# Fused attention and two FFNs on one core: weight conversion begins every second step, and the early FFN products of two token blocks come in two parts

## The chip, the core and the metric

One core of a Trainium2 chip runs the whole program once per launch. Its engines work beside each other, each through its own instructions in order: TensorE (PE; its weight loads are PEld), VectorE (DVE), ScalarE (ACT), GpSimd (POOL), and SyncE (SP), which here issues every DMA. The metric is the device time of one execution in microseconds (us).

## What is computed

Local-and-global attention, then two feed-forward networks one behind the other, on 4 x 544 tokens of 512 features (cut to what matters):

```python
# attention: 32 global and 512 local tokens, 8 heads of 64, window 32
out_g = sm(scale * q_g @ [k_g, k_l].T) @ [v_g, v_l]
out_l = sm(concat(scale * q_l @ k_g.T, masked(scale * q_l @ k_l.T))) @ [v_g, v_l]
x = concat(out_g, out_l)                    # 2176 tokens x 512
# first FFN, 512 -> 2048 -> 512
x = (max(x @ w_in1, 0) ** 2) @ w_out1
# second FFN, a quotient of polynomials between its products
h = x @ w_in2
g = (a0 + a1*h + a2*h**2 + a3*h**3) / (1 + abs(b0)*abs(h) + abs(b1)*h**2 + 1e-6)
out = g @ w_out2
```

The four FFN weights arrive as float64. Each is turned into two float32r words, a high part and a rest, so that three products stand for one of higher precision.

## The kernel before, in words

**Weight items.** The weights are cut into chunks f = 0 to 15 of 128 hidden features; an item is one half (in or out) of a chunk of one FFN: 64 items, 512 KB each as loaded. `w_load` (line 107) loads one into a buffer S; then `w_abs` (ACT, line 150) writes a buffer T, `w_low` (POOL) scales the low words, and DVE does `w_clamp` (153), `w_shift` (164), `w_sign` (168) and `w_add` (173). An item that stays in SBUF then gets `w_hi` (ACT cast, 186) and `w_lo` (DVE, 193); an item of mode "word" is only written from T to a DRAM scratch by a DMA (line 178). The first 10 items (chunks 0 to 4 of the first FFN, NPRE = 5) stay; the next 12 are of mode "word". These 22 are done during attention. S has three buffers in the pool cvp, and items 3 to 6 take four more that borrow the space of weight chunks 3 and 4. T has four buffers in the pool cv3.

**Ticks.** `cv_tick` (line 237) is the clock of this conversion. Every call adds one to a counter and to the age of each item in work. When the counter reaches `cv["per"]` a new item's load is issued; each operation is issued when the item's age reaches the number in the table OX or OE. Attention runs over steps i = 0 to 40, each ending with some ticks: four up to step 14, from then on 2 + i % 2. With per = 4, one item begins in each of the steps 0 to 14, and later one in 1.6 steps.

**Attention steps.** There are eight half-batches (n = 0 to 7: batch and four heads) of five groups. Step i issues, in order: exponentials (747) of group i + 2, scores `do_S` (733, 754) of group i + 3 with their DVE reductions (739), transposes of q and k for the next half-batch (`prep`, 700), the transposition of probabilities `do_T` (787), the transposition of results into xT (`do_xT`, 853), the product with v (`do_PV`, 827), and the ticks. Loads of q, k and v for later half-batches are issued on SP at fixed positions of a step; the v windows of a half-batch are then shifted by four SBUF-to-SBUF copies (lines 601 to 604).

**Fill jobs.** From step F0 = 11 on, one job of the first FFN goes with each step, to keep TensorE filled: 30 jobs, for six blocks of 256 tokens (a) with the five resident chunks (f). `f_h` (507) does the 12 products of the first matrix, `f_low` the square's rest on DVE, `f_y` (529) the 12 products of the second, one step later, summed in two PSUM banks. At the last chunk of a block both banks are copied to T buffers (line 544, one copy on DVE and one on ACT) and written to a DRAM tensor `park` (545). `f_split` (496) makes the two parts of a block of x, four pairs of an ACT cast and a DVE subtraction (503, 504). Job (a, f) can begin when both items of chunk f are done.

**FFN stage.** After attention, `step` (line 440) runs the rest of both FFNs; the parked sums are read back and added.

**Order.** The schedule is written by hand: each engine runs its instructions in the order of issue above, so a waiting instruction holds up all that stands behind it on its engine. SP issues loads, copies and stores in one such line.

Of the kernel before, what the change touches and what calls it, by code (L numbers as in the profile page):

```python
# [23 lines left out]
def kernel(  # L24
# [19 lines left out]
    T = SL + SG  # L44
# [4 lines left out]
    NK = DM // 128  # L49
# [4 lines left out]
    NPRE, NPART, NSUB = 5, 1536, 256  # L54
# [6 lines left out]
    pe, ve, sc, gp, sy = nc.tensor, nc.vector, nc.scalar, nc.gpsimd, nc.sync  # L61
# [25 lines left out]
    cv3 = ctx.enter_context(tc.tile_pool(name="cv3", bufs=4))  # L87
# [7 lines left out]
    park = drp.tile([128, NK, NPART], F32, name="park")  # L95

    def w_src(ap, ph, half, f, m):

        if half:
            return [(slice(0, 128), ap[f * 128:(f + 1) * 128, :])]  # L100
        c = ap[:, f * 128 * m:(f + 1) * 128 * m]
        if ph:
            return [(slice(0, 128), c.rearrange("(k p) f -> p k f", p=128))]
        v = c.rearrange("(u h d) f -> u d h f", u=2, d=D)
        return [(slice(64 * u, 64 * u + 64), v[u]) for u in range(2)]

    def w_load(it):

        ph, f, half = it["k"]
        ap = ((w_in1, w_out1), (w_in2, w_out2))[ph][half]  # L110
        if it["mode"] == "wide":

            if cv["n"] in (3, 5):
                x = wpre.tile([128, 2, 2, 512], F32R, tag=("w4", "w3")[cv["n"] // 5], name="S4").bitcast(U32)
                cv["S"] = [x[:, z].rearrange("p a c -> p (a c)").rearrange("p (a b) -> p a b", b=2) for z in (1, 0)]
            if 3 <= cv["n"] < 7:
                t = cv["S"].pop()
            else:
                t = cvp.tile([128, 512, 2], U32, tag="S", name="S")
            cv["n"] += 1  # L120
            it["S"] = t
            dst, m = t.rearrange("p a b -> p (a b)"), 2
            ap = ap.bitcast(U32)
        else:
            t = cv3.tile([128, 512], U32, tag="T", name="T").bitcast(F32)
            it["T"] = t
            dst, m = t, 1
            if wide:
                sy.dma_start(dst, scr[ph, f, half])
                return  # L130
        for rows, src in w_src(ap, ph, half, f, m):
            d = dst[rows]
            sy.dma_start(d if half else d.rearrange("p (k f) -> p k f", k=NK), src)
# [89 lines left out]

    OX = dict(abs=8, elow=8, clamp=9, shift=9, sign=9, add=10, hi=16, lo=18)
    OE = dict(abs=4, elow=4, clamp=5, shift=6, sign=6, add=8, hi=11, lo=13)
    OL = dict(abs=2, low=3, clamp=3, shift=4, sign=4, add=5, hi=7, lo=9)
    OS = dict(hi=5, lo=8)
    ORD = ("hi", "add", "lo", "clamp", "shift", "sign", "low", "elow", "abs")  # L230
# [256 lines left out]
    fs = ctx.enter_context(ExitStack())  # L487
# [2 lines left out]
    def fill(i):  # L490
        return fp.tile([128, (10, 4, 2)[i] * NSUB], F32, tag=f"f{i}", name=f"f{i}")

    frows, fturn, fx, fh, fg, fy = [], dict(x=0, h=0), {}, {}, {}, []
    fjobs = [(a, f) for a in range(NPART // NSUB) for f in range(NPRE)]

    def frow(i, r):
        return frows[i][:, NSUB * r:NSUB * r + NSUB]

    def f_split(a, k):
        i = fturn["x"] = (fturn["x"] + 1) % 5  # L500
        hi, lo = [frow(0, 2 * i + z).bitcast(F32R) for z in range(2)]
        src = xT[:, k, NSUB * a:NSUB * a + NSUB]
        sc.copy(hi, src)
        ve.tensor_tensor(out=lo, in0=src, in1=hi.bitcast(F32), op=ALU.subtract)
        fx[a, k] = hi, lo

    def f_h(q):
        a, f = fjobs[q]
        while (0, f, 1) not in done:
            cv_tick(LEFT[1])  # L510
        w, h = wt[0, f], bank("H")[:, 0:NSUB]
        for m, (k, s, t) in enumerate([(k, s, t) for k in range(NK) for s, t in ((0, 0), (1, 0), (0, 1))]):
            pe.matmul(h, w[:, s, 0, 128 * k:128 * k + 128], fx[a, k][t], start=m == 0, stop=m == 3 * NK - 1)  # L513
        if f == NPRE - 1:
            for k in range(NK):
                fx.pop((a, k))
        i = fturn["h"] = (fturn["h"] + 1) % 2
        hi, lo = [frow(1, 2 * i + z).bitcast(F32R) for z in range(2)]
        g = frow(2, i)
        sc.activation(g, h, AF.Relu)  # L520
        sc.activation(hi, g, AF.Square)
        fh[q], fg[q] = (hi, lo), (g, h)
# [4 lines left out]
        ve.tensor_tensor(out=lo, in0=g, in1=hi.bitcast(F32), op=ALU.subtract)  # L527

    def f_y(q):
        a, f = fjobs[q]  # L530
        hi, lo = fh.pop(q)
        w = wt[0, f]
        if f == 0:
            fy[:] = [bank("Y"), bank("Y")]
        ms = range(NK)
        for m, z in [(m, z) for m in ms for z in range(2)] + [(m, 2) for m in ms]:

            pe.matmul(fy[m // 2][:, NSUB * (m % 2):NSUB * (m % 2) + NSUB], w[:, z % 2, 1, 128 * m:128 * m + 128],  # L538
                      (hi, hi, lo)[z], start=f == 0 and z == 0 and m % 2 == 0, stop=f == NPRE - 1 and z == 2,
                      skip_group_check=True)  # L540
        if f == NPRE - 1:
            for i in range(2):
                t = cv3.tile([128, 512], U32, tag="T", name="pk").bitcast(F32)
                (sc.copy if i else ve.tensor_copy)(t, fy[i])
                sy.dma_start(park[:, 2 * i:2 * i + 2, NSUB * a:NSUB * a + NSUB], t.rearrange("p (m t) -> p m t", m=2))


    with ExitStack() as at:
# [69 lines left out]
        for i, pair in enumerate(some):  # L618
            for h in range(4):
                p, m = slice(32 * h, 32 * h + 32), pair[h % 2]  # L620
# [18 lines left out]
        def load_g(i):  # L639
            sy.dma_start(gr[i].rearrange("g (x d) -> g x d", d=D), (q_g, k_g)[i].rearrange("b h g d -> g (b h) d"))  # L640

        for c in "kGqAgKQB":
            if c in "qk":
                load_qk(0, "qk".index(c))
            elif c in "QK":
                load_qk(1, "QK".index(c))
            elif c in "gG":
                load_g("gG".index(c))
            else:
                load_v(0, "ABR".index(c))  # L650
# [61 lines left out]
        F0 = 11  # L712
# [151 lines left out]
        pend = {}  # L864
        cv["at"] = OX

# [11 lines left out]
        for i in range(NS + 1):  # L878
# [4 lines left out]
            for c in (LD0 if n == 0 else LD)[pos] if i < NS else ():  # L883
                if c in "qk":
                    m = n + 2 + (c == "k" and pos == 4)
# [34 lines left out]
            if fq == -1:  # L920
                for k in range(NK):
                    f_split(0, k)
            elif 0 <= fq < len(fjobs) - NPRE:
                a, f = fjobs[fq]
                for k in range(NK):
                    if f == (NPRE - 1 if k else NPRE - 2):
                        f_split(a + 1, k)
            if i == 0:
                prep_g(0)
            if i == 1:  # L930
# [1 line left out]
                sy.dma_start(coef[:, 4:6], b2.rearrange("(o a) -> o a", o=1).to_broadcast([128, 2]))  # L932
            if i == 10:
                sc.activation(coef[:, 6:8], coef[:, 4:6], AF.Abs)
            if i == F0 + NPRE - 1:
                cv["at"] = OE
            for _ in range(4 if i < F0 + NPRE - 1 else 2 + i % 2):
                cv_tick(LEFT[1])
        do_xT(NS - 1)
        f_y(len(fjobs) - 1)  # L940
# [43 lines left out]
```

## Time and profile before

| | us |
|---|---|
| median of 3 runs | 942.24 (941.53 to 942.43) |
| the profiled execution | 942.59 |
| its span, first to last instruction | 940.8 |
| PE busy in the span | 903.2 (96%) |
| DVE busy | 727.1 (77%) |
| ACT busy | 618.5 (66%) |

The span is a little shorter than the execution; 1.8 us lie around it. Busy shares are means over stages with different limits, so the rows below are taken by stage: a row of stage times gives the stretch, then for each engine the busy time and, in brackets, the count of instructions, then the granted share of the TensorE clock, the mean busy share of the 16 DMA engines and what they moved. Engine names with a q (SPq) are of the engine's instruction queue. A note such as [1.44 <-DMA kr] tells for how long the engine had been idle and what released it.

### The profile page before, as it was taken

Reading aid. Unit: us, or ns where it says so; the run is one execution under the profiler, and the core shown is the slowest. Engines: PE = TensorE matmul, PEld = TensorE weight load, DVE = VectorE, ACT = ScalarE, POOL = GpSimd, SP = SyncE. Lnnn points to the kernel's source line nnn. Section 1 sums busy time; section 2 is a strip of 40 time slices with the busy share of each in tenths; the row PEclk is TensorE's granted clock in tenths of the full one; section 3 lists DMA queues with packets and bytes.
Section 4 is the critical chain, followed back from the end, with each engine's and each line's share of the span. In section 5 each row is a group of like instructions: output and inputs, shape, how many; then the busy total and the mean of one; then the engine's idle time right before and its main releaser. Section 6 shows DMA issues by size and latency. Waiting matters only on the chain.

```text
span 940.8 us, 19428 instructions
## 1 busy us (share of the span) xinstructions
PE 903.2 (96%) x7440; PEld 822.5 (87%) x7440; DVE 727.1 (77%) x1731; ACT 618.5 (66%) x1323; POOL 57.7 (6%) x109
## 2 busy tenths in 40 slices
PE   7878889999999999999999999999999999999997
PEld 4657788898999999999999988889889998988875
DVE  3599887765469577586766569989989999989886
ACT  3567475654578554555554557877888788787886
POOL 5233122210000000000000000000000000000000
PEclk9888999999999999999999999999999999999999
DMA  9997788730365264354522540010010010010000
GB/s 177 187 216 166 179 213 204 174 104 25 93 177 157 71 188 157 126 200 157 155 82 79 167 147 1 1 33 1 1 34 1 1 34 1 1 34 1 25 10 23
DMA packets 104301, 89.45 MB, mean 95 GB/s; under 512 B 60176, under 2 KB 87312, under 8 KB 104208
## 3 DMA queue, kind: packets, MB, share of 16 engines
q1 hardware_dynamic: 104208, 88.21, 35.2%
q8 instruction: 58, 0.95, 0.4%
q14 instruction: 35, 0.29, 0.1%
HBM read 62.13 MB, written 19.14 MB: 86 GB/s over the span
## 4 chain that ended last, share of the span: by engine, by line
PE 81%; DVE 10%; ACT 4%; DMA 3%; issue 1%; SPq 1%; ACTq 0%; DVEq 0%
PE S L314 33%; PE y L394 18%; PE y L391 15%; PE H L513 4%; PE Y L538 3%; PE S L733 2%; PE tr L700 1%; PE PV L827 1%; DVE T L168 1%; PE T L787 1%; DVE s L739 1%; DVE T L173 1%; DMA S<-in_moe_w_in_dram 1%; DMA big<-in_v_l_dram 1%; DVE tq L364 1%
## 5 line engine op out<-in xcount | busy, mean ns | idle before, releaser
L314 PE MATMUL S<-big,w 128*128 128x384 f32 (+1 forms) x1776 | 328.8, 326 | 2.1 <-ACT big L296 1.1
L314 PEld LDWEIGHTS S<-big,w 128*128 128x128 f32 x1776 | 296.5, 188 | 9.2 <-DVE ts L354 2.2
L394 PE MATMUL y<-w,big 128*128 128x512 f32 x816 | 209.1, 398 | 4.2 <-ACT big L372 2.9
L394 PEld LDWEIGHTS y<-w,big 128*128 128x128 f32 x816 | 149.3, 188 | 38.2 <-DVE big L373 8.1
L391 PE MATMUL y<-big,w 128*128 128x384 f32 (+1 forms) x912 | 159.6, 324 | 0.6 <-DVE xT L401 0.6
L391 PEld LDWEIGHTS y<-big,w 128*128 128x128 f32 x912 | 149.2, 188 | 1.5 <-DVE xT L401 1.0
L350 ACT ACTIVATE big<-S 128x384 f32<-128x384 f32 (+1 forms) x96 | 45.6, 475 | 75.4 <-PE S L314 72.1
L329 ACT ACTIVATE big<-S 128x384 f32<-128x384 f32 (+1 forms) x76 | 35.6, 468 | 81.9 <-PE S L314 81.9
L337 DVE TENSOR_TENSOR big<-big 128x384 f32<-128x384 f32 (+1 forms) x60 | 31.3, 522 | 71.2 <-ACT big L333 71.2
L353 DVE TENSOR_TENSOR ts<-ts,S 128x384 f32<-128x384 f32 (+1 forms) x96 | 50.9, 530 | 24.3 <-ACT ts L351 24.2
L314 PE MATMUL S<-xm,w 128*128 128x384 f32 (+1 forms) x288 | 67.8, 328 | 0.0
L352 ACT ACTIVATE tq<-big,coef 128x384 f32<-128x384 f32 (+1 forms) x96 | 66.1, 689 | 0.0
L351 ACT ACTIVATE ts<-S,coef 128x384 f32<-128x384 f32 (+1 forms) x96 | 62.5, 651 | 0.0
L354 DVE SCALAR_TENSOR_TENSOR ts<-ts,coef,S 128x384 f32<-128x384 f32 (+1 forms) x96 | 56.9, 593 | 3.4
L333 ACT ACTIVATE big<-big 128x384 fp32r<-128x384 f32 (+1 forms) x76 | 38.3, 504 | 29.6 <-PE y L391 29.1
L314 PEld LDWEIGHTS S<-xm,w 128*128 128x128 f32 x288 | 52.1, 188 | 2.9
L150 ACT ACTIVATE T<-S 128x512 f32<-128x512 f32 x64 | 42.7, 670 | 17.9 <-DMA S<-in_moe_w_in_dram 8.9
L366 DVE SCALAR_TENSOR_TENSOR ts<-tq,ts 128x384 f32<-128x384 f32 (+1 forms) x96 | 51.4, 536 | 3.3
L538 PE MATMUL Y<-f,w 128*128 128x256 f32 x360 | 51.3, 293 | 0.0
L513 PE MATMUL H<-f,w 128*128 128x256 f32 x360 | 51.0, 291 | 0.0
L373 DVE TENSOR_TENSOR big<-ts,big 128x384 fp32r<-128x384 f32 (+1 forms) x96 | 50.8, 529 | 0.2 <-ACT big L372 0.2
L355 DVE TENSOR_TENSOR tq<-tq,big 128x384 f32<-128x384 f32 (+1 forms) x96 | 50.8, 529 | 0.0
(131 smaller groups left out, 1314.2 us busy)
## 6 DMA issues: line engine op xcount, KB each, us to landing
S<-in_moe_w_out_dram SPq DMA_DIRECT2D x32, 512.0 KB, 4.5
S<-in_moe_w_in_dram SPq DMA_DIRECT2D x32, 256.0 KB, 4.5
S<-in_moe_w_in_dram SPq DMA_DIRECT2D x16, 512.0 KB, 4.5
scr<-T SPq DMA_DIRECT2D x24, 256.0 KB, 3.2
T<-scr SPq DMA_DIRECT2D x24, 256.0 KB, 2.7
both<-stg SPq DMA_DIRECT2D x10, 512.0 KB, 3.5
w<-both SPq DMA_DIRECT2D x10, 512.0 KB, 4.4
out_dram<-xT SPq DMA_DIRECT2D x17, 256.0 KB, 2.6
```

The costliest lines, as they stand in the source:

```text
L314: pe.matmul(h, wk[k][s], x[k][t], start=m == 0, stop=m == 3 * NK - 1)
L351: sc.activation(s, h, AF.Identity, scale=coef[:, 3:4], bias=coef[:, 2:3])
L352: sc.activation(q, av, AF.Identity, scale=coef[:, 7:8], bias=coef[:, 6:7])
L353: ve.tensor_tensor(out=s, in0=s, in1=h, op=ALU.mult)
L354: ve.scalar_tensor_tensor(out=s, in0=s, scalar=coef[:, 1:2], in1=h, op0=ALU.add, op1=ALU.mult)
L355: ve.tensor_tensor(out=q, in0=q, in1=av, op=ALU.mult)
L366: ve.scalar_tensor_tensor(out=s, in0=q, scalar=2.0, in1=s, op0=ALU.subtract, op1=ALU.mult, reverse0=True)
L373: ve.tensor_tensor(out=lo, in0=s, in1=hi.bitcast(F32), op=ALU.subtract)
L391: pe.matmul(y[m][:, 0:n], a, x, start=st and z == 0, stop=sp and z == 2)
L394: pe.matmul(y[m], a, x, start=st and z == 0, stop=sp and z == 2)
L513: pe.matmul(h, w[:, s, 0, 128 * k:128 * k + 128], fx[a, k][t], start=m == 0, stop=m == 3 * NK - 1)
L538: pe.matmul(fy[m // 2][:, NSUB * (m % 2):NSUB * (m % 2) + NSUB], w[:, z % 2, 1, 128 * m:128 * m + 128], (hi, hi, lo)[z], start=f == 0 and ...
```

## The change

- Items begin every second step up to step 8 (`per=8`, counter started at 4): items 0 to 4 in steps 0, 2, 4, 6, 8; from then one in each of steps 9 to 13, and from step 14 one in seven ticks. All steps have four ticks. The tables OX and OE get shorter ages, and OE holds from step 11. The last item's load is issued in step 34 instead of 25.
- The four borrowed S buffers go; all items use the three of cvp.
- Fill jobs come in segments: blocks 0 and 1 with chunks 0 and 1 first, then block 0 and block 1 with chunks 2 to 4, then blocks 2 to 5 with all five. For the second parts of blocks 0 and 1 the parked sums are loaded into T buffers while their last `f_h` is issued, added to the PSUM banks on DVE, and written again. x of blocks 0 and 1 is split twice.
- At the start, k of the second half-batch (K) and the four v copies (B) are issued ahead of the load of q_g (g) and of the second q (Q).

```diff
@@ w_load
-            if cv["n"] in (3, 5):
-                x = wpre.tile([128, 2, 2, 512], F32R, tag=("w4", "w3")[cv["n"] // 5], name="S4").bitcast(U32)
-                cv["S"] = [x[:, z].rearrange("p a c -> p (a c)").rearrange("p (a b) -> p a b", b=2) for z in (1, 0)]
-            if 3 <= cv["n"] < 7:
-                t = cv["S"].pop()
-            else:
-                t = cvp.tile([128, 512, 2], U32, tag="S", name="S")
-            cv["n"] += 1
+            t = cvp.tile([128, 512, 2], U32, tag="S", name="S")
...
-    todo, line, cv = [], [], dict(z=0, n=0, at=None, per=4, lo=ve)
+    todo, line, cv = [], [], dict(z=4, at=None, per=8, lo=ve)
...
-    OX = dict(abs=8, elow=8, clamp=9, shift=9, sign=9, add=10, hi=16, lo=18)
-    OE = dict(abs=4, elow=4, clamp=5, shift=6, sign=6, add=8, hi=11, lo=13)
+    OX = dict(abs=8, elow=8, clamp=9, shift=9, sign=9, add=10, hi=13, lo=14)
+    OE = dict(abs=4, elow=4, clamp=5, shift=5, sign=5, add=6, hi=9, lo=10)
...
-    fjobs = [(a, f) for a in range(NPART // NSUB) for f in range(NPRE)]
+    segs = [(0, (0, 1), False), (1, (0, 1), False), (0, (2, 3, 4), True), (1, (2, 3, 4), True)]
+    segs += [(a, range(NPRE), False) for a in range(2, NPART // NSUB)]
+    fjobs = [(g, a, f, f == fs[0], f == fs[-1], add) for g, (a, fs, add) in enumerate(segs) for f in fs]
...
@@ f_h
-        if f == NPRE - 1:
+        if last:
             for k in range(NK):
-                fx.pop((a, k))
+                fx.pop((seg, k))
+            if add:
+                for i in range(2):
+                    t = cv3.tile([128, 512], U32, tag="T", name="pk").bitcast(F32)
+                    sy.dma_start(t.rearrange("p (m t) -> p m t", m=2), f_park(a, i))
+                    fpk.append(t)
...
@@ f_y
-        if f == NPRE - 1:
+        if last:
             for i in range(2):
-                t = cv3.tile([128, 512], U32, tag="T", name="pk").bitcast(F32)
-                (sc.copy if i else ve.tensor_copy)(t, fy[i])
-                sy.dma_start(park[:, 2 * i:2 * i + 2, NSUB * a:NSUB * a + NSUB], t.rearrange("p (m t) -> p m t", m=2))
+                if add:
+                    t = fpk.pop(0)
+                    ve.tensor_tensor(out=t, in0=fy[i], in1=t, op=ALU.add)
+                else:
+                    t = cv3.tile([128, 512], U32, tag="T", name="pk").bitcast(F32)
+                    (sc.copy if i else ve.tensor_copy)(t, fy[i])
+                sy.dma_start(f_park(a, i), t.rearrange("p (m t) -> p m t", m=2))
...
-        for c in "kGqAgKQB":
+        for c in "kGqAKBgQ":
...
@@ the attention steps
-            elif 0 <= fq < len(fjobs) - NPRE:
-                a, f = fjobs[fq]
-                for k in range(NK):
-                    if f == (NPRE - 1 if k else NPRE - 2):
-                        f_split(a + 1, k)
+            elif 0 <= fq:
+                for d, ks in ((1, range(1, NK)), (2, range(1))):
+                    if fq + d < len(fjobs) and fjobs[fq + d][3]:
+                        for k in ks:
+                            f_split(fq + d, k)
...
-            if i == F0 + NPRE - 1:
+            if i == F0 - 3:
+                cv.update(z=0, per=4)
+            if i == F0:
                 cv["at"] = OE
-            for _ in range(4 if i < F0 + NPRE - 1 else 2 + i % 2):
+            if i == F0 + 3:
+                cv["per"] = 7
+            for _ in range(4):
                 cv_tick(LEFT[1])
```

## Rows read from the trace of the kernel before

**Rows 1.** Stage times: stretch, length, PE PEld DVE ACT POOL busy, clock, DMA, GB/s.

```profile
26.50:40.70 14.20, 13.42 (x220) 9.71 (x222) 6.98 (x34) 8.19 (x25) 2.91 (x5) 0.76 0.83 167
40.70:75.60 34.90, 27.57 (x536) 20.33 (x537) 33.40 (x109) 22.76 (x58) 11.14 (x15) 0.85 1.05 217
75.60:124.20 48.60, 41.05 (x657) 35.51 (x658) 42.00 (x129) 30.66 (x82) 14.24 (x17) 0.93 0.76 175
124.20:165.30 41.10, 38.94 (x652) 34.30 (x649) 31.36 (x112) 24.28 (x65) 8.40 (x11) 1.00 0.84 210
165.30:242.20 76.90, 76.90 (x1337) 69.26 (x1337) 49.49 (x196) 42.37 (x118) 8.67 (x10) 1.00 0.35 91
249.00:940.80 691.80, 681.37 (x3792) 636.40 (x3790) 553.87 (x1098) 478.42 (x950) 0.00 (x0) 1.00 0.23 73
```

**Rows 2.** Chain of waits, shares by line, stretches 40.7 to 75.6 and 165.3 to 242.2.

```profile
by line: DMA big<-in_v_l_dram 18.0%; DMA S<-in_moe_w_out_dram 13.3%; DVE T L168 9.5%; DVE T L173 8.5%; SPq L570 6.3%; DVE s L739 5.6%; SPq L133 5.5%; DVE T L164 5.2%; DVE T L153 5.1%; DVE w L193 3.4%; issue 3.2%; PE S L733 3.2%; DVE xs L838
...
by line: PE H L513 30.2%; PE Y L538 28.6%; PE PV L827 9.2%; PE S L733 7.9%; PE T L787 6.2%; PE tr L700 4.6%; PE PV L832 4.2%; PE tr L853 3.7%; PE S L754 2.1%; PE T L798 1.7%; PE tr L803 0.9%; PE S L758 0.7%
```

**Rows 3.** Stage times of line 168 alone (DVE `w_sign`): one instruction for each item.

```profile
40.70:75.60 34.90, 5.38 (x7) 0.85 1.05 217
75.60:124.20 48.60, 5.50 (x7) 0.93 0.76 175
...
165.30:242.20 76.90, 2.09 (x3) 1.00 0.35 91
```

**Rows 4.** Stage times of line 193 alone (DVE `w_lo`).

```profile
40.70:75.60 34.90, 3.56 (x5) 0.85 1.05 217
75.60:124.20 48.60, 4.26 (x5) 0.93 0.76 175
```

**Rows 5.** Groups by line, whole span: count, busy, mean ns, idle before.

```profile
L168 DVE SCALAR_TENSOR_TENSOR T<-S,T 128x512 uint32<-128x512 uint32 x64 | 45.9, 717 | 2.2
...
L173 DVE CUSTOM_DVE_ANT_0 T<-S,T 128x1024 uint16<-128x1024 uint16 x64 | 45.7, 714 | 3.5 <-DVE T L168 0.5
...
L193 DVE TENSOR_TENSOR w<-T,w 128x512 fp32r<-128x512 f32 x54 | 37.3, 704 | 4.0 <-ACT w L186 4.0
...
L164 DVE TENSOR_SCALAR T<-T 128x512 uint32<-128x512 uint32 x64 | 29.0, 454 | 0.9
...
L153 DVE TENSOR_SCALAR T<-T 128x512 f32<-128x512 f32 x64 | 28.7, 450 | 10.9 <-ACT T L150 10.9
...
L504 DVE TENSOR_TENSOR f<-xT,f 128x256 fp32r<-128x256 f32 x24 | 9.0, 418 | 0.2 <-ACT f L503 0.2
L399 DVE TENSOR_TENSOR xT<-y,xT 128x384 f32<-128x384 f32 x16 | 8.0, 549 | 0.0
...
L544 DVE COPY pk<-Y 128x512 f32<-128x512 f32 x6 | 4.1, 688 | 2.4 <-PE Y L538 2.4
```

**Rows 6.** Timeline: the first v copies and what SP issues ahead of them.

```profile
12.43 0.43 SPq L640 DMA_DIRECT2D gr<-in_q_g_dram  x1
...
15.15 2.30 SPq L570 DMA_DIRECT2D raw<-in_q_l_dram  x4
...
19.49 0.60 SPq L604 DMA_DIRECT2D big<-big  x1
...
24.21 0.32 PE L827 MATMUL PV<-big,pt 128*32 128x65 f32 x8 [1.85 <-DMA big<-big]
25.97 0.51 PE L827 MATMUL PV<-big,pt 128*32 128x65 f32 x8 [1.44 <-DMA kr<-in_k_l_dram]
```

**Rows 7.** Timeline: a `w_abs` that waits for a T buffer.

```profile
115.01 0.90 SPq L545 DMA_DIRECT2D park<-pk  x2
...
117.29 0.66 ACT L150 ACTIVATE T<-S 128x512 f32<-128x512 f32 x1 [4.28 <-DMA park<-pk]
...
119.69 1.11 PE L853 MATMUL tr<-ident,xs 128*128 128x128 f32 x4 [2.84 <-ACT kt L708]
```

**Rows 8.** Waits of ACT, 0 to 249 us: total, times, longest.

```profile
ACT T L150 <- DMA S<-in_moe_w_in_dram: 2.4, 2, 1.3
```

**Rows 9.** DMA issues: count, KB each, median us to landing.

```profile
S<-in_moe_w_out_dram SPq DMA_DIRECT2D x32, 512.0 KB, 4.5
```

More of the change, by code (lines that the diff above doesn't have):

```diff
@@ L491, in fill, with f_split @@
         return fp.tile([128, (10, 4, 2)[i] * NSUB], F32, tag=f"f{i}", name=f"f{i}")
-    frows, fturn, fx, fh, fg, fy = [], dict(x=0, h=0), {}, {}, {}, []
-    fjobs = [(a, f) for a in range(NPART // NSUB) for f in range(NPRE)]
+    frows, fturn, fx, fh, fg, fy, fpk = [], dict(x=0, h=0), {}, {}, {}, [], []
+    segs = [(0, (0, 1), False), (1, (0, 1), False), (0, (2, 3, 4), True), (1, (2, 3, 4), True)]
+    segs += [(a, range(NPRE), False) for a in range(2, NPART // NSUB)]
+    fjobs = [(g, a, f, f == fs[0], f == fs[-1], add) for g, (a, fs, add) in enumerate(segs) for f in fs]
     def frow(i, r):
         return frows[i][:, NSUB * r:NSUB * r + NSUB]
-    def f_split(a, k):
+    def f_split(q, k):
+        g, a = fjobs[q][:2]
         i = fturn["x"] = (fturn["x"] + 1) % 5
@@ L504, in f_split, with f_park @@
         ve.tensor_tensor(out=lo, in0=src, in1=hi.bitcast(F32), op=ALU.subtract)
-        fx[a, k] = hi, lo
+        fx[g, k] = hi, lo
+    def f_park(a, i):
+        return park[:, 2 * i:2 * i + 2, NSUB * a:NSUB * a + NSUB]
     def f_h(q):
-        a, f = fjobs[q]
+        seg, a, f, _, last, add = fjobs[q]
         while (0, f, 1) not in done:
@@ L512, in f_h @@
         for m, (k, s, t) in enumerate([(k, s, t) for k in range(NK) for s, t in ((0, 0), (1, 0), (0, 1))]):
-            pe.matmul(h, w[:, s, 0, 128 * k:128 * k + 128], fx[a, k][t], start=m == 0, stop=m == 3 * NK - 1)
-        if f == NPRE - 1:
+            pe.matmul(h, w[:, s, 0, 128 * k:128 * k + 128], fx[seg, k][t], start=m == 0, stop=m == 3 * NK - 1)
+        if last:
             for k in range(NK):
-                fx.pop((a, k))
+                fx.pop((seg, k))
[4 more added lines that the diff above has]
+                    fpk.append(t)
         i = fturn["h"] = (fturn["h"] + 1) % 2
@@ L529, in f_y @@
     def f_y(q):
-        a, f = fjobs[q]
+        _, a, f, first, last, add = fjobs[q]
         hi, lo = fh.pop(q)
         w = wt[0, f]
-        if f == 0:
+        if first:
             fy[:] = [bank("Y"), bank("Y")]
@@ L538, in f_y @@
             pe.matmul(fy[m // 2][:, NSUB * (m % 2):NSUB * (m % 2) + NSUB], w[:, z % 2, 1, 128 * m:128 * m + 128],
-                      (hi, hi, lo)[z], start=f == 0 and z == 0 and m % 2 == 0, stop=f == NPRE - 1 and z == 2,
+                      (hi, hi, lo)[z], start=first and z == 0 and m % 2 == 0, stop=last and z == 2,
                       skip_group_check=True)
-        if f == NPRE - 1:
+        if last:
             for i in range(2):
-                t = cv3.tile([128, 512], U32, tag="T", name="pk").bitcast(F32)
-                (sc.copy if i else ve.tensor_copy)(t, fy[i])
-                sy.dma_start(park[:, 2 * i:2 * i + 2, NSUB * a:NSUB * a + NSUB], t.rearrange("p (m t) -> p m t", m=2))
+                if add:
[5 more added lines that the diff above has]
+                sy.dma_start(f_park(a, i), t.rearrange("p (m t) -> p m t", m=2))
     with ExitStack() as at:
```

## The prediction

> **What bounds the kernel now.** I read the stage times first [rows 1]: the reader is to compare each stage's busy times with its length. From 249 us on PE is busy for 681.37 of 691.80 us, and nothing of the change runs there (the 22 items are converted, the six blocks parked, before it begins), so the FFN stage is taken as it is. The same holds, with one difference, from 165.3 to 242.2: PE has no idle time, and the chain of waits is PE alone [rows 2]. So the change can win only in the first 165 us.
>
> There the limit changes by stage. From 40.7 to 75.6 (attention steps 4 to 10) DVE is busy for 33.40 of 34.90 us, PE for 27.57 at a granted clock of 0.85, that is about 23.4 us if all of it ran at full clock. The chain of this stretch [rows 2] goes through the weight items' DVE lines (168, 173, 164, 153, 193) and through DMAs, of v and of an item. DMA moves 217 GB/s here, the most of any stage shown, at a busy share of 1.05 [rows 1]. So DVE bounds, with DMA close behind, and both are loaded by weight items: seven pass through `w_sign` and five through `w_lo` in this stage [rows 3, 4]. From 75.6 to 124.2 (steps 11 to 17) DVE is busy for 42.00 of 48.60 and PE for 41.05, and part of the rest is one event: a `w_abs` waited 4.28 us for a T buffer, its ACT queue with it, and PE lost 2.84 us [rows 7]. From 124.2 to 165.3 PE is idle for only 41.10 - 38.94 = 2.16 us.
>
> **The start (steps 0 and 1).** The products with v in step 0 wait 1.85 and 1.44 us for the v copies, the last of which is issued at 19.49 [rows 6]. The new order takes two issues from ahead of them, 0.43 and 2.30 us, so they can go 2.73 us earlier. They read the v loads, and SP must wait until those have landed; if that binds at once, nothing is won. Ends: -2.7 and 0. I take -2.2, near the first, since the PE idle time that it eats, 3.29 us, is larger. q_g and the second q go behind and are used after these products. Behind this wait the clock falls: 26.5 to 40.7 has a granted clock of 0.76, which is 14.2 x 0.24 / 0.5 = 6.8 us at the 1.2 GHz level [rows 1], worth at most 3.4 us of PE work. A shorter wait may keep the 2.4 GHz level; I take -1.0 out of 0 to -3.4. The Trainium skill (TensorE: Matmul & The Clock Gate, What's actually happening) says that "the default state is throttled, and activity releases the throttle"; by that rule the whole 3.4 us could come back, which is in the second rival.
>
> **Steps 4 to 10.** Ticks issued in one step are run by DVE about at the next, so this stage sees the ticks of steps 3 to 9: after the change items 0 to 3 with their four operations and 0 to 2 with their low half, against seven and five. One item costs 450 + 454 + 717 + 714 ns = 2.34 us on DVE, its low half 0.70 [rows 5]. Removed: 3 x 2.34 + 2 x 0.70 = 8.4 us, which leaves 33.40 - 8.4 = 25.0 us of DVE. At the density of now (33.40 / 34.90 = 0.957) that is 26.1 us: -8.8. The other end is DMA. The stage moves 217 GB/s x 34.9 us = 7.57 MB. An item is 512 KB [rows 9]; two fewer loads are issued in these steps (five, not seven) and two fewer just before. With two gone and no more than 217 GB/s it takes 30.0 us (-4.9), with all four 25.2 (-9.7). I take -8.0, near the DVE end, because SP, which issues in one line, also gets the two earlier loads' time.
> The Trainium skill (DMA: Bandwidth & Descriptors, Specifications) puts the HBM limit of a core at about 358 GB/s; no row here comes near it, so the measured 217 decides, and by the page's figure DMA would bound nothing and this term would be -8.8.
>
> **Steps 11 to 17.** What was taken out returns in part here. Items 4 to 10 pass (seven, as now), but seven low halves instead of five: +1.4. x is split 12 times instead of 4: 8 x 0.418 = +3.3 on DVE. The first parts of both blocks are parked here, one DVE copy more: +0.7 [rows 5]. That makes 42.00 + 5.4 = 47.4 us, at 0.957 49.5: +0.9. The load is also uneven: the ticks of step 13 hold two items and a low half (5.4 us) in a step for which PE needs some 5.5 with attention's own DVE work beside it; I add 1. The T event of [rows 7] does not go, it moves: when block 0's first part is parked, in step 13, items 5, 6 and 7 hold three of the four T buffers, so of the two copies the second, on ACT, must wait for the first one's DMA to DRAM; behind it on ACT stand the next casts and exponentials. By the row, 4.28 us of such a wait cost PE 2.84; it takes the place of the same event now in steps 16 and 17: net 0. Sum +2, ends -2 (the moved event is hidden by the DVE work beside it) and +8 (both add up).
>
> **Steps 18 to 24.** At most the 2.16 us of PE idle time can go. Added are four adds from PSUM: 549 ns for 384 columns is an estimate of 732 ns for 512, between that row and the 688 of the copy [rows 5]: 2.9 us less one copy, with one item less; DVE comes to some 33 of 39 us and is covered by PE. Added on SP and DMA are four loads of parked sums and two more stores, 256 KB each, 1.57 MB: 210 GB/s x 41.1 = 8.63 MB becomes 10.2, at 217 GB/s 47.0 us, +5.9 if DMA set the pace. Ends -2.2 and +5.9. I take 0: q, k and v are loaded some steps ahead, and the next stage has a DMA share of 0.35 [rows 1], so a lag can be made up.
>
> **Steps 25 to 39.** Seven items instead of three pass [rows 3]: 4 x 2.34 = 9.4 us more on DVE, 58.9 of 76.9. PE covers it; for short peaks I take +0.5, ends 0 and +2. The last item is done in step 37, ahead of the FFN stage; were it not, the remaining ticks would run before that stage.
>
> **Sum.** -2.2 - 1.0 - 8.0 + 2.0 + 0 + 0.5 = -8.7. Against the profiled execution, 942.59, that is 933.9; the median of the runs is 0.35 lower, so 933.5.
>
> **Rivals.** (1) DMA sets the pace: steps 4 to 10 win 4.9, steps 18 to 24 lose a third of their bound, 2. For it: the share of 1.05 and the DMAs on the chain [rows 1, 2]. Against: DVE's 96%. -2.2 - 1.0 - 4.9 + 2 + 2 + 0.5 = -3.6: 938.6. (2) Everything evens out: the clock stays at its upper level and the short stalls vanish: -2.7 - 3.4 - 9.7 + 0 - 2.2 + 0.5 = -17.5: 924.7. (3) Gain given back: the dense steps 11 to 17 cost 8 and the parked loads 2: -0.7, 941.5, no change. (4) Slower, by the short lead of the loads. From item 7 on the load is four ticks, one step of some 5 us, ahead of its `w_abs`; a load takes 4.5 us to land [rows 9] behind its issue and whatever stands before it on SP. Now the lead is two steps, later 1.6, and ACT waited 2.4 us in all for such loads of the in half [rows 8]. If a load is late, ACT stops with the exponentials behind it. By [rows 7] the first 4.28 - 2.84 = 1.4 us of an ACT wait are free. For 15 items (7 to 21), waits of 2.2 us each would cost 15 x 0.8 = 12 us: 945.5. It decides against the change from about 2.0 us each, when 15 x 0.6 eats the 8.7. Against it: ACT is busy for only 59% of steps 18 to 24.
>
> **How the numbers follow.** Forecast 0.54, rivals 0.17, 0.13, 0.07 and 0.09. The likeliest case by itself spans 929 to 937.5. The range of 8 in 10 leaves out the slower rival, most of (3) and the far half of (2): 925.5 to 940.2. A change under about 0.2%, 1.9 us, can't be told from none. Faster by more: 0.84; within: 0.08; slower: 0.08.
>
> **What would show it.** Right: steps 4 to 10 take 25 to 28 us; DVE is still over 90% busy in steps 11 to 17 and these are no shorter than now; PE has no idle time in the later ones; the half-batch copies release step 0 some 2 us earlier. Wrong: the T waits of ACT on S loads grow over some 10 us in total (rival 4), DMA near 217 GB/s with DVE idle in steps 4 to 10 (rival 1), or PE idle time behind step 25.

## The result and the profile after

The changed kernel takes 950.22 us (median of 10 runs, 942.83 to 952.63); the kernel before takes 942.26 on the same chip (10 runs, 939.72 to 946.1). The ratio is 1.0063, interval 1.0038 to 1.0089: slower by less than 1%, outside the predicted range. In another set of runs the same changed kernel took 944.93 against 943.04, ratio 1.0020 (1.0007 to 1.0033). The two intervals don't touch, and why is not settled. So the change costs between 0.2 and 0.6%, where 0.9% of gain was forecast.

The profiled execution took 951.82 us, with a span of 950.0: 9.2 us more than in the span before. The first table compares stages. A stage ends with the last product with v of its last step.

| steps | before | after | difference | predicted | after, second profile |
|---|---|---|---|---|---|
| 0 to 3 | 40.7 | 35.3 | -5.4 | -3.2 | 35.1 |
| 4 to 10 | 34.8 | 27.8 | -7.0 | -8.0 | 27.4 |
| 11 to 17 | 48.7 | 57.8 | +9.1 | +2.0 | 56.4 |
| 18 to 24 | 41.0 | 41.8 | +0.8 | 0 | 44.1 |
| 25 to 39 | 76.9 | 84.4 | +7.5 | +0.5 | 83.0 |
| end of step 39 | 242.2 | 247.1 | +4.9 | -8.7 | 246.1 |
| from there on | 698.6 | 702.9 | +4.3 | 0 | 698.6 |

The early stages gave what was forecast, -12.4 us instead of -11.2. Then 17.4 us were lost in three stages for which 2.5 had been put down. The last line is a thing apart: nothing of the change runs there, and the second profile of the same program (the run e8_again below) shows 698.6, as before.

The stage times of the kernel after, which answer to [rows 1] (stretch, length, busy PE, PEld, DVE, ACT, POOL, granted clock, DMA share, GB/s):

```profile
21.90:35.30 13.40, 12.62 (x220) 9.22 (x222) 6.88 (x34) 8.19 (x25) 3.95 (x5) 0.87 0.83 161
35.30:63.10 27.80, 23.24 (x536) 17.38 (x535) 23.33 (x96) 19.84 (x56) 6.66 (x9) 0.94 1.04 204
63.10:120.90 57.80, 44.68 (x663) 37.61 (x666) 44.67 (x140) 32.67 (x88) 10.42 (x14) 0.85 0.75 160
120.90:162.70 41.80, 38.67 (x649) 34.24 (x648) 33.10 (x110) 23.81 (x64) 10.55 (x13) 0.98 0.84 217
162.70:247.10 84.40, 79.50 (x1339) 70.81 (x1337) 59.20 (x212) 44.86 (x122) 12.03 (x15) 0.97 0.47 125
253.90:950.00 696.10, 684.71 (x3792) 639.92 (x3790) 553.87 (x1098) 478.43 (x950) 0.00 (x0) 1.00 0.23 73
```

Steps 4 to 10 have DVE at 23.33 us instead of 33.40 and a clock of 0.94. Steps 11 to 17 are 9 us longer with hardly more DVE work (44.67 against 42.00): DVE is now idle for 13 us of a stage in which it was to be the bound. Of the 5.4 us of DVE work that had been put down there, 2.7 came. PE is idle there for 57.80 - 44.68 = 13.1 us, 5.6 more than before, and busy 3.6 us longer, since the clock is 0.85 instead of 0.93. In steps 25 to 39, where PE had no idle time at all, it has 84.40 - 79.50 = 4.9, and 2.6 us more of busy time at a clock of 0.97.

**Where steps 11 to 17 lose.** Of PE's 13.1 idle us, half are in step 14, which takes 13.9. Its timeline (start, duration, engine, line, operation, count, idle time before and what released it):

```profile
84.24 6.43 SPq L552 DMA_DIRECT2D park<-pk  x2
85.72 3.05 POOL L606 COPY vw<-vw 32x1040 f32<-32x1040 f32 x3
...
89.70 0.59 ACT L551 COPY pk<-Y 128x512 f32<-128x512 f32 x1 [7.17 <-DMA park<-pk]
90.18 0.41 ACT L498 CAST f<-xT 128x256 fp32r<-128x256 f32 x1
...
90.62 0.42 DVE L499 TENSOR_TENSOR f<-xT,f 128x256 fp32r<-128x256 f32 x1 [6.52 <-ACT f L498]
90.96 0.75 DVE L145 TENSOR_SCALAR T<-T 128x512 f32<-128x512 f32 x2
91.63 0.75 DVE L156 TENSOR_SCALAR T<-T 128x512 uint32<-128x512 uint32 x2
92.31 1.28 DVE L160 SCALAR_TENSOR_TENSOR T<-S,T 128x512 uint32<-128x512 uint32 x2
...
93.51 1.28 DVE L165 CUSTOM_DVE_ANT_0 T<-S,T 128x1024 uint16<-128x1024 uint16 x2
...
96.89 1.10 PE L839 MATMUL PV<-big,pt 96*32 96x65 f32 x32 [5.33 <-DVE xs L845]
```

Read it from the bottom. PE waits 5.33 us for `xs`, the scaling of an earlier product. DVE computes that after the operations of two weight items, which stand ahead of it. These start only at 90.96, for DVE had stood still for 6.52 us behind a split of x, whose cast is on ACT; and ACT waited 7.17 us for a T buffer, held by the first copy of the parked sums until its DMA had landed. That store is issued at 84.24, after four v copies on SP (at 82.39 and 83.20 the last two), and the wait ends 5.4 us later.

**Where steps 25 to 39 lose.** The waits of ACT, 0 to 249 us (total, times, longest), which answer to [rows 8]; first one of the kernel before that [rows 8] leaves out, then those of the kernel after:

```profile
ACT T L150 <- DMA S<-in_moe_w_out_dram: 1.4, 1, 1.4
```

```profile
ACT T L142 <- DMA S<-in_moe_w_out_dram: 12.3, 6, 3.4
...
ACT T L142 <- issue: 6.9, 2, 3.4
...
ACT T L142 <- DMA S<-in_moe_w_in_dram: 6.5, 3, 3.2
```

`w_abs` (line 142 now) waits 12.3 + 6.5 = 18.8 us for loads, where it waited 2.4 + 1.4 = 3.8. Of the 18.8 us, 10.3 lie in steps 11 to 17 and 6.5 in steps 25 to 39. The two waits put down to "issue" (3.44 and 3.42 us, in steps 24 and 28) are of the same kind as far as the trace tells: POOL's `w_low` of the same item starts 0.1 us later, and its wait is put down to the load. So ACT stands still for some 13 us for late loads in steps 18 to 39. One such wait, in step 33:

```profile
203.97 0.90 SPq L552 DMA_DIRECT2D park<-pk  x2
...
204.97 0.45 SPq L125 DMA_DIRECT2D S<-in_moe_w_out_dram  x1
...
209.86 0.67 ACT L142 ACTIVATE T<-S 128x512 f32<-128x512 f32 x1 [3.36 <-DMA S<-in_moe_w_out_dram]
209.94 0.67 POOL L150 TENSOR_SCALAR S<-S 128x512 uint32<-128x512 uint32 x1 [15.30 <-DMA S<-in_moe_w_out_dram]
...
210.68 3.65 POOL L606 COPY vw<-vw 32x1040 f32<-32x1040 f32 x3
...
211.02 1.16 DVE L156 TENSOR_SCALAR T<-T 128x512 uint32<-128x512 uint32 x1
...
212.21 1.42 DVE L160 SCALAR_TENSOR_TENSOR T<-S,T 128x512 uint32<-128x512 uint32 x1
...
213.76 1.10 DVE L165 CUSTOM_DVE_ANT_0 T<-S,T 128x1024 uint16<-128x1024 uint16 x1
...
216.32 1.09 PE L834 MATMUL PV<-big,pt 128*32 128x65 f32 x32 [3.14 <-DVE xs L845]
```

The load is issued behind a store of parked sums, and ACT stands still until 209.86. POOL's queue waits for the same load: `w_low` starts at 209.94, and the v copies that stand behind it follow at 210.68. So the late load sets free at one moment the item's DVE operations and POOL's copies, next to which they take 1.16, 1.42 and 1.10 us; in [rows 5] they have 0.45, 0.72 and 0.71. PE then waits 3.14 us for `xs`. Other places where PE waits are steps 24 (2.66 us) and 28 (1.24).

### The profile page after: what moved, and what is told of

Read it like the earlier page. It is cut to its first block, busy times and chain, and to the rows that moved or that the text cites. A ratio compares the mean times of both kernels' runs of the same rounds, so it can differ in the third digit from the quotient of the medians.

```text
span 950.0 us, 19472 instructions
## 1 busy us (share of the span) xinstructions
PE 906.0 (95%) x7440; PEld 824.9 (87%) x7440; DVE 731.0 (77%) x1743; ACT 619.6 (65%) x1331; POOL 56.0 (6%) x109
## 4 chain that ended last, share of the span: by engine, by line
PE 76%; DVE 7%; DMA 6%; ACT 6%; issue 2%; SPq 1%; ACTq 0%; DVEq 0%
PE S L306 31%; PE y L386 18%; PE y L383 13%; PE H L511 3%; DMA S<-in_moe_w_out_dram 3%; PE Y L541 3%; DMA S<-in_moe_w_in_dram 2%; PE tr L707 1%; PE S L740 1%; PE PV L834 1%; PE PV L839 1%; DVE T L160 1%; PE T L794 1%; DVE T L165 1%; DMA vw<-vw 1%
## 5 line engine op out<-in xcount | busy, mean ns | idle before, releaser
L325 ACT ACTIVATE big<-big 128x384 fp32r<-128x384 f32 (+1 forms) x76 | 38.2, 503 | 30.2 <-PE y L383 29.7
```

## The experiments

Two theories for the loss: the **T pool**, that is the copy of parked sums that waits for a T buffer in step 14, and the **short lead** of the loads behind step 18. A third, suggested by step 33, is the **v copies** of POOL beside the weight items. A fourth is that the **parts** themselves cost more than they cover.

| run | ratio to before, same chip | median us | steps 4 to 10 | 11 to 17 | 18 to 39 |
|---|---|---|---|---|---|
| before | | 942.26 beside the change, 943.2 beside e1 to e4, 943.04 beside e5 to e8, 944.16 beside e9 and e10 | 34.8 | 48.7 | 118.0 |
| the change | 1.0063 (1.0038 to 1.0089) | 950.22 | 27.8 | 57.8 | 126.2 |
| e8_again | 1.0020 (1.0007 to 1.0033) | 944.93 | 27.4 | 56.4 | 127.1 |
| e1_pk | 0.9993 (0.9971 to 1.0016) | 942.82 | 29.7 | 50.3 | 129.3 |
| e2_lead | 0.9978 (0.9954 to 1.0001) | 940.97 | 28.4 | 54.1 | 120.7 |
| e3_order | 0.9980 (0.9958 to 1.0002) | 941.51 | 37.0 | 48.6 | 118.4 |
| e4_whole | 0.9957 (0.9938 to 0.9977) | 939.28 | 27.6 | 52.6 | 122.5 |
| e7_nopool | 0.9971 (0.9955 to 0.9987) | 940.67 | 26.5 | 55.7 | 119.5 |
| e5_even | 0.9939 (0.9915 to 0.9963) | 938.18 | 32.8 | 51.8 | 117.3 |
| e9_both | 0.9925 (0.9898 to 0.9952) | 937.08 | 29.7 | 50.0 | 122.9 |
| e6_wholeeven | 0.9886 (0.9853 to 0.9920) | 933.26 | 32.8 | 47.2 | 115.0 |
| e10_again | 0.9890 (0.9868 to 0.9913) | 932.86 | 33.5 | 47.8 | 115.5 |

**e1_pk: the first parked copies get a buffer of their own** (that of a weight chunk not yet in use).

```diff
-                    t = cv3.tile([128, 512], U32, tag="T", name="pk").bitcast(F32)
+                    if fjobs[q][0] == 0:
+                        if i == 0:
+                            pk4 = wpre.tile([128, 2, 2, 512], F32R, tag="w4", name="pk4").bitcast(F32)
+                        t = pk4[:, i, 0]
+                    else:
+                        t = cv3.tile([128, 512], U32, tag="T", name="pk").bitcast(F32)
```

> The two T buffers of the first parked segment (step 13) lie in the free space of chunk 4's weights, so that the second copy needn't wait for the first one's DMA. If the full T pool made the loss of steps 11 to 17 (57.8 us against 48.7 before), ACT's wait of 7.17 us at the park copy and PE's waits of 5.33 and 1.24 us in step 14 go, steps 11 to 17 take 49 to 52 us and the time falls by 6 to 8 us. If the dense weight work on DVE made it (rival), the wait only changes its name and the time falls by under 2 us.

ACT's wait for the park store is gone, and steps 11 to 17 take 50.3 us, 7.5 less. But step 14 still takes 11.5, and PE still waits 5 us in it. The timeline of step 14, columns as above:

```profile
86.03 3.82 POOL L611 COPY vw<-vw 32x1040 f32<-32x1040 f32 x3
...
86.17 2.99 DVE L160 SCALAR_TENSOR_TENSOR T<-S,T 128x512 uint32<-128x512 uint32 x2
...
89.08 1.92 DVE L165 CUSTOM_DVE_ANT_0 T<-S,T 128x1024 uint16<-128x1024 uint16 x2
...
93.09 1.09 PE L844 MATMUL PV<-big,pt 96*32 96x65 f32 x32 [5.11 <-DVE xs L850]
```

The two items now meet POOL's v copies: four of their operations take 2.99 + 1.92 us instead of 1.28 + 1.28. So the T wait is a cause, and worth 7.5 us of the 9.1 in this stage; the step with two items is still long without it, but the stage is now only 1.6 us longer than before. Steps 18 to 24 came out 4.1 us longer than in the first profile of the change (1.8 longer than in the second), so only part of the 7.5 us reached the end.

**e2_lead: the load is issued three ticks more ahead of `w_abs` from the fourth fill step on.**

```diff
+    OW = dict(abs=7, elow=7, clamp=8, shift=8, sign=8, add=9, hi=12, lo=13)
...
-                cv["per"] = 7
+                cv.update(per=7, at=OW)
```

> From item 10 on all ages are three ticks longer (abs 7, add 9, hi 12), so a load has seven ticks of lead instead of four; nothing else changes. If the short lead made the losses of steps 18 to 39 (126.2 us against 118.0), ACT's waits for S loads (18.8 us in attention) fall under 6 us, steps 18 to 39 take 118 to 121 us, and the time falls by 5 to 8 us. If the cause is more DVE work in these steps or the parked adds (rival), they stay within 2 us.

ACT's waits for loads, 0 to 249 us, and its wait for the T buffer:

```profile
ACT pk L552 <- DMA park<-pk: 9.0, 1, 9.0
...
ACT T L142 <- DMA S<-in_moe_w_out_dram: 5.0, 3, 3.3
...
ACT T L142 <- DMA S<-in_moe_w_in_dram: 1.8, 3, 1.3
```

18.8 us of load waits are down to 6.8, a little over the 6 expected, and none of them lies in steps 18 to 39 (two put down to "issue", 5.3 us, are left there). These take 120.7 us instead of 126.2, while the T wait and the long step 14 (16.05 us) are still there. So the longer lead gives back 5.5 of the 8.2 us that these steps had lost. In step 33 it also parts POOL's copies from the item's work; the copies and the item's first DVE operation there:

```profile
203.67 3.05 POOL L607 COPY vw<-vw 32x1040 f32<-32x1040 f32 x3
...
207.78 0.42 DVE L145 TENSOR_SCALAR T<-T 128x512 f32<-128x512 f32 x1
```

Whether it is the wait of ACT or the meeting with the copies that costs, this run doesn't tell; e7_nopool does.

**e3_order: the kernel before with the new order of its first loads alone.**

```diff
-        for c in "kGqAgKQB":
+        for c in "kGqAKBgQ":
```

> The kernel before with the new order of the first loads alone (K and the v copies ahead of q_g and Q). If the start's gain stands by itself, step 0 ends 4 to 5 us earlier and the time falls by 3 to 5 us. If DVE, which bounds steps 4 to 10 with its weight items, gives it back (rival), the time stays within 1 us.

Step 0 ends at 22.47 instead of 26.48 and steps 0 to 3 are 4.8 us shorter, so the order accounts for most of the 5.4. But with the old density of items, steps 4 to 10 take 37.0 instead of 34.8, and at the end of step 39 2.4 us are left. Their stage time:

```profile
35.90:72.90 37.00, 27.23 (x535) 19.72 (x537) 33.90 (x110) 22.06 (x58) 14.30 (x16) 0.86 1.07 220
```

DVE has the same 33.9 us of work as before, DMA moves 220 GB/s at a share of 1.07. ACT's `w_abs` waits 12.7 us for loads in this stage, where it waited 2.5 in the kernel before: what starts earlier runs into the loads. By the times 1.7 us are won, and the interval just includes no change.

**e4_whole: the change with the token blocks whole, not in parts.**

```diff
-    segs = [(0, (0, 1), False), (1, (0, 1), False), (0, (2, 3, 4), True), (1, (2, 3, 4), True)]
-    segs += [(a, range(NPRE), False) for a in range(2, NPART // NSUB)]
+    segs = [(a, range(NPRE), False) for a in range(NPART // NSUB)]
```

> The change without the parts: all six blocks with five chunks each, as before, with the change's late items; a job whose chunk isn't ready issues the missing ticks first. If the parts are what covers the late chunks, PE waits for weights at steps 13 to 15 and steps 11 to 17 take 58 to 64 us, the time is equal or up to 6 us longer. If the parts themselves are the cost (more splits, parking twice), steps 11 to 17 take 50 to 54 us and the time falls by 4 to 8 us.

Steps 11 to 17 take 52.6 us, where the change takes 57.8 and 56.4. The parts do cover something, as PE's waits from 60 to 249 us show; without them its jobs wait for the low half of a chunk:

```profile
PE H L510 <- DVE w L185: 7.8, 3, 5.3
```

There is no such wait in the change. But what the parts bring with them (eight more splits, four more stores, four loads, and T buffers held in the fullest stage, with the T wait) costs more than it saves: the kernel is faster without them, 0.9957 against 1.0063 and 1.0020, the intervals not touching. ACT waits even longer for loads here than in the change (25.0 us in all), and yet steps 18 to 39 are shorter, 122.5 us: the sum of such waits doesn't by itself give the loss.

**e7_nopool: POOL's copies of the global v rows left out from the third half-batch on.**

```diff
+                if n > 1:
+                    return
```

> The change without the GpSimd copies of the global v rows into the windows from the third half-batch on (they are left out: the rows of an earlier half-batch stay). In the change, DVE's w_shift and w_sign took 1.16 and 1.42 us beside these copies, 0.43 and 0.70 elsewhere. If the two engines slow each other, these go back to 0.45 and 0.72, the stalls of steps 14, 24 and 33 shrink by 1 to 2 us each, and the time falls by 3 to 6 us. If the DVE times have another cause, nothing moves by more than 1 us.

Ratio 0.9971, so 4.3 us less than the change on the same chip; steps 18 to 39 take 119.5 us instead of 127.1. The shift and the sign of DVE by shape, 60 to 235 us (count, busy, mean ns, idle before), first in the change and then here:

```profile
L160 DVE SCALAR_TENSOR_TENSOR T<-S,T 128x512 uint32<-128x512 uint32 x19 | 14.8, 785 | 0.6
L156 DVE TENSOR_SCALAR T<-T 128x512 uint32<-128x512 uint32 x19 | 10.1, 534 | 0.6
```

```profile
L160 DVE SCALAR_TENSOR_TENSOR T<-S,T 128x512 uint32<-128x512 uint32 x18 | 12.4, 694 | 0.6
...
L156 DVE TENSOR_SCALAR T<-T 128x512 uint32<-128x512 uint32 x18 | 8.0, 449 | 0.6
```

Without the copies beside them the two operations go back to the values of an undisturbed one. Step 33 in this run:

```profile
203.93 0.68 ACT L142 ACTIVATE T<-S 128x512 f32<-128x512 f32 x1 [3.32 <-DMA S<-in_moe_w_out_dram]
...
205.11 0.43 DVE L156 TENSOR_SCALAR T<-T 128x512 uint32<-128x512 uint32 x1
...
205.57 0.69 DVE L160 SCALAR_TENSOR_TENSOR T<-S,T 128x512 uint32<-128x512 uint32 x1
...
206.40 0.69 DVE L165 CUSTOM_DVE_ANT_0 T<-S,T 128x1024 uint16<-128x1024 uint16 x1
...
208.54 0.66 PE L836 MATMUL PV<-big,pt 128*32 128x65 f32 x32 [1.24 <-DVE xs L847]
```

ACT waits for the load as long as in the change, 3.32 us, but PE waits 1.24 us instead of 3.14. The load waits are all still there (17.0 us in all, 18.8 in the change), and steps 18 to 39 are only 1.5 us longer than in the kernel before. So late loads alone cost little here; with POOL's copies set free beside the item's work they cost 8 to 9 us. e2_lead and this run take away much of the same loss from its two ends, so their gains can't be added. The T wait of step 14 is as long as ever (8.9 us) and so is the step. All DMAs are still there, and among PE's waits in the change (60 to 249 us) none is for these copies, so as far as the rows tell it is their meeting with DVE's work that costs: 4.3 us by the times, 7.6 by the profiles of steps 18 to 39.

**e8_again: the change once more, beside e5 to e7.**

> The change once more, for the part of its loss that lies behind attention: in its profile the FFN stage took 4.3 us longer than in the profile before, with 4.24 instead of 4.16 us for each job of the first FFN, while four kernels with the same FFN code took 1.7 to 2.9 more than before. If that is the change's own doing, its FFN stage is again over 4 us longer; if it varies between executions, it lies at 1 to 3 us, and the loss is that of attention, about 5 us.

It was run because the stretch behind attention had been 4.3 us longer in the first profile. Here that stretch is as before:

```profile
252.90:944.60 691.70, 681.24 (x3792) 636.72 (x3790) 554.16 (x1098) 478.47 (x949) 0.00 (x0) 1.00 0.23 73
```

691.70 us with 681.24 of PE, against 696.10 with 684.71 in the first and 691.80 with 681.37 in [rows 1]. The instructions are the same in all three. The other nine runs lie between: from the end of step 39 on they take 699.1 to 701.6 us, with the same code in this stretch, against 698.6 here and 702.9 in the first profile. So of the 9.2 us in the first profile only 4.9 belong to the change, and 3.9 in the second; the medians of the two sets of runs, +8.0 and +1.9 us, lie on either side. What makes this stretch longer in one execution than in another stays open.

**e9_both: the edits of e1_pk and e2_lead together.**

> The change with two of its waits taken away together: the first parked sums in the space of chunk 4's weights (as in e1_pk) and the long lead from item 10 on (as in e2_lead). If the two losses are separate, steps 11 to 17 take about 50 us and steps 18 to 39 about 121, and the time falls by 8 to 12 us against the change, to 934 to 938. If one hides the other, no more is won than by e2_lead alone (within 2 us of it).

937.08 us, ratio 0.9925. Steps 11 to 17 take 50.0 us and steps 18 to 39 122.9: the first is as in e1_pk (50.3), the second 2.2 us longer than in e2_lead, so by the stages the gains add up but for 2.2 us. Step 14 still takes 12.1 us and has the longest wait of PE between 60 and 235 us:

```profile
PE PV L845 <- DVE xs L851: 5.7, 1, 5.7
```

So with both waits mended, the step with two items remains.

**e5_even: items 4 to 9 begin earlier, one in each step, and later ones with the long lead.**

```diff
+    OW = dict(abs=7, elow=7, clamp=8, shift=8, sign=8, add=9, hi=12, lo=13)
...
-            if i == F0 - 3:
+            if i == F0 - 4:
                 cv.update(z=0, per=4)
-            if i == F0:
-                cv["at"] = OE
-            if i == F0 + 3:
-                cv["per"] = 7
+            if i == F0 + 2:
+                cv.update(per=7, at=OW)
```

> The change with its items spread evenly: one a step already from step 7 (items 4 to 9 in steps 7 to 12), all ten with the longer table OX, so that no step holds two items' work and only two of them hold T buffers when the first sums are parked in step 13; and from item 10 on the long lead of e2_lead. If the full T pool, the doubled step 13 and the short lead are the causes, steps 11 to 17 take 48 to 52 us (57.8 in the change), steps 18 to 39 118 to 121, and the time falls by 10 to 14 us against the change, under the kernel before. If the parts of the FFN products cost by themselves, steps 11 to 17 stay over 54 us.

938.18 us, ratio 0.9939: 6.8 us less than the change on the same chip, where 10 to 14 were expected. Steps 18 to 39 take 117.3, as in the kernel before. Steps 4 to 10 give back 5 us of their gain. The store of the parked sums holds up no copy on ACT any more, and step 14 takes 8.1 us instead of 13.9 to 16.1; but `w_abs` now waits for a T buffer in steps 14 and 15 (5.5 and 3.4 us), and step 15 takes 11.1 us instead of 7.3, at a granted clock of 0.65. With 51.8 us the stage is no better than with two items in one step and the T wait mended (50.3 and 50.0 in e1_pk and e9_both). So no run here shows a share of the crowded step by itself; the longer lead from step 13 on and the even start together take away the loss of the later stages.

**e6_wholeeven: e4_whole, an even start of the items and the long lead together.**

```diff
+    OW = dict(abs=7, elow=7, clamp=8, shift=8, sign=8, add=9, hi=12, lo=13)
...
-    segs = [(0, (0, 1), False), (1, (0, 1), False), (0, (2, 3, 4), True), (1, (2, 3, 4), True)]
-    segs += [(a, range(NPRE), False) for a in range(2, NPART // NSUB)]
+    segs = [(a, range(NPRE), False) for a in range(NPART // NSUB)]
...
-            if i == F0 - 3:
+            if i == 5:
                 cv.update(z=0, per=4)
-            if i == F0:
-                cv["at"] = OE
-            if i == F0 + 3:
-                cv["per"] = 7
+            if i == 12:
+                cv.update(per=7, at=OW)
```

> No parts: whole blocks, items 0, 1, 2 in steps 0, 2, 4, then one a step from step 5 (item 9 in step 11), long lead from item 10 on. Steps 4 to 10 have more DVE work than in the change (26 to 31 us), steps 11 to 17 fewer splits and no double step: 46 to 52 us. If the parts are worth their work, this is slower than e5_even by 2 to 4 us; if they are not, it is equal or faster.

933.26 us, ratio 0.9886 (0.9853 to 0.9920): faster than both kernels. Its stage times from step 4 on:

```profile
35.40:68.30 32.90, 22.90 (x539) 17.14 (x537) 27.33 (x102) 20.46 (x55) 9.18 (x12) 0.95 1.03 208
68.30:115.40 47.10, 42.60 (x655) 36.52 (x655) 41.17 (x128) 30.19 (x81) 10.61 (x13) 0.89 0.77 163
115.40:153.40 38.00, 38.00 (x652) 33.90 (x648) 30.42 (x107) 24.20 (x65) 10.53 (x13) 1.00 0.95 211
153.40:230.40 77.00, 76.97 (x1341) 69.29 (x1337) 56.17 (x208) 44.64 (x121) 11.03 (x14) 1.00 0.50 128
```

From step 18 on PE is busy for 114.97 of 115.00 us, although the last stage holds 56.17 us of DVE work, almost as much as the change's 59.20. The work added there was not the loss; its timing was. ACT still waits 10.4 us for loads in all (6.9 + 3.5), and no longer for a store:

```profile
ACT T L142 <- DMA S<-in_moe_w_in_dram: 6.9, 4, 2.4
...
ACT T L142 <- DMA S<-in_moe_w_out_dram: 3.5, 2, 2.4
```

**e10_again: e6_wholeeven once more, on another chip.**

> e6_wholeeven once more, with more runs: whole blocks, items spread evenly, long lead. If its gain is that of attention, the time is 8 to 12 us under the kernel before and the attention stage ends at 229 to 233 us.

932.86 us, ratio 0.9890 (0.9868 to 0.9913): the gain is confirmed. Step 39 ends at 230.05 and 230.41 in the two profiles, 11.8 to 12.2 us before that of the kernel before.

## Why the prediction was wrong, point by point

- **What bounds the kernel: right for steps 4 to 10.** DVE did hold them: with the items thinned out it is busy for 23.33 us (25.0 forecast, items and low halves 4 and 3 as counted), and the stage is 7.0 us shorter (8.0 forecast). At the same time its share fell from 96 to 84%, at a DMA share of 1.04: both are then close to the limit, as the first rival had it, and the stage is 0.9 us longer than the 26.9 forecast.
- **The start: right in kind, too small.** -2.2 and -1.0 were taken, -4.6 and -0.8 came, and -3.2 and -2.4 in the second profile. The granted clock of steps 1 to 3 rose from 0.76 [rows 1] to 0.87, and to 1.00 in the second profile. The prediction put both waits of the products with v down to the v copies; [rows 6] names the load of k for the 1.44 us. It bounded the gain by 2.73 us, but the last v copy went out at 14.73 instead of 19.49. SP was also done earlier with the v loads ahead of it (10.41 instead of 12.38), whose order is the same; why, the runs don't show. Step 0 ended between 21.07 and 24.66 us in the runs with this order, though its code is the same in all; a term of this size can't be read from one profile to better than some 2 us.
- **Steps 11 to 17: the first step that failed, the "net 0" for the moved T wait.** The prediction saw the event: the second copy of parked sums, on ACT, waiting for the store of the first. It called it "net 0", as it would take the place of the one in [rows 7], and let +1 stand for the dense step. In the old event too DVE stood still behind ACT, for 3.00 us, with one item behind it; 4.28 us of wait cost PE 2.84. DVE's row of the kernel before:

```profile
117.98 0.43 DVE L153 TENSOR_SCALAR T<-T 128x512 f32<-128x512 f32 x1 [3.00 <-ACT T L150]
```

The new one lies in the step with two items and the splits of x. ACT's wait is 7.17 us, and DVE needs ACT's cast, so it stood still for 6.52 us with two items queued, which then ran ahead of `xs`: 6.6 us of PE idle time in step 14 alone, and a lower clock of the stage (0.85 instead of 0.93). The upper end of +8 was meant for this ("both add up"), and +9.1 and +7.7 came. e1_pk sizes the failed term: without the T wait the stage takes 50.3 us, 7.5 less, and 1.6 more than before, close to the +1.9 that had been put down for the added work and the dense step together. e4_whole shows that the parts as a whole don't pay.
- **The store was part of that.** The prediction put no time on it. In the kernel before, a park store lands 2.4 us after its issue in the median; in the place where it counts, the wait ended 5.4 us after the issue, and the issue itself came after four copies on SP.
- **Steps 18 to 24: about right.** 0 was taken and +0.8 came (+3.1 in the second profile). The prediction's "some 33 us" of DVE work doesn't follow from its own terms, which give 31.36 + 2.9 - 0.7 - 2.34 = 31.2; 33.10 came. DMA moved 217 GB/s there without setting the pace: e2_lead moved 241 GB/s in about the same stage (its stage time, columns as above):

```profile
116.90:158.50 41.60, 38.82 (x652) 34.13 (x649) 33.84 (x115) 24.86 (x68) 8.92 (x11) 1.00 0.93 241
```

So 217 GB/s, from which the first rival and the upper end of this term were worked out, was not the most that DMA gives in this stage.

- **Steps 25 to 39: the second step that failed.** "PE covers it" holds for the work, as e6_wholeeven shows, but not for work that comes late. The +0.5 for it measured +7.5 (+6.1 in the second profile). The fourth rival had half of the mechanism: the lead of one step against 4.5 us for a load [rows 9], and ACT waits of 2 us and more. It named a growth of over 10 us in such waits as its sign, and 18.8 us came, 15.0 more than before. It was given 0.09 because ACT is busy for only 59% of its time. As far as ACT alone goes that held: with the same waits but without POOL's copies, steps 18 to 39 lose 1.5 us (e7_nopool). What neither the forecast nor the rival saw is that POOL's queue waits for the same load, so that the v copies come free together with the item's DVE operations and slow them, in front of the `xs` that PE needs.
- **The rival's price** was 12 us over 15 items; e2_lead recovered 5.5. That the total came close to its 945.5 (944.93 and 950.22) is luck: the T event and the copies, which it didn't price, added what was missing.
- **What was to show it.** Steps 4 to 10 at 27.8 us and the earlier step 0 were right. Load waits of ACT over 10 us and idle PE time behind step 25 told against the forecast, as named. DVE was to be over 90% busy in steps 11 to 17 and was 77% busy; this is the simplest sign of the error: a stage taken to be bound by one engine's work lost its time to waits in a queue.

## What to carry to other kernels

When work is moved in a hand-ordered schedule, price the waits at the new place, not at the old one: list what stands behind the waiting instruction on its engine, then what the next engine has queued, and add these up unless a row shows them side by side. Then ask what else a late event sets free at the same moment: late loads alone cost 1.5 us in steps 18 to 39, and 8 to 9 us where they let POOL's copies and DVE's work start together. Busy shares speak for an engine's work, not for its order. Spreading the items evenly with a long lead and whole blocks paid here (0.989), where the thinning with a short lead, a crowded step and blocks in parts cost (1.002 to 1.006).

## What the runs showed of the hardware

- **DVE beside POOL's copies.** In step 33 of the change POOL makes three copies in 3.65 us, about 1.22 each with the gaps; in step 14, where DVE stood still, three took 3.05. DVE's shift begins at 211.02, in the first copy, and ends at 212.18; the first copy ends at about 210.68 + 1.22 = 211.90. The sign and the add end in the same way about half a microsecond behind the second and third copy. They take 1.16, 1.42 and 1.10 us; in the same step of e7_nopool, without the copies, 0.43, 0.69 and 0.69. So each of the three ends only behind a copy, three times in a row. The Trainium skill (SBUF — State Buffer, SBUF: two separate sides) says that the port pair which VectorE and GpSimd share is "an exclusive lock, not a bandwidth split"; this trace agrees in that an operation begun in a copy ends only behind it, for the shift with one input as for the sign with two. It doesn't show that all of the operation waited: the shift ends 0.28 us behind the copy and takes 0.43 alone.
- **A stretch that is the same work at another pace.** The time behind attention was 4.4 us longer in one execution of the change than in another (696.10 against 691.70), with PE busy 3.5 us longer at the same granted clock of 1.00. The other runs lie between the two, and none tells why.
- **DMA.** e2_lead moved 241 GB/s over 41.6 us at a share of 0.93, more than the 217 at a share of 1.05 in [rows 1]: a share of 1 is no fixed number of bytes.
